# Attention with QK norm and a maxout FFN: two-part row loads, five turning products, regrouped values and an alternating spread in the first six head pairs, with the second pair's norms in the opening

## Chip, cores and metric

One Trainium2 chip, one core. The time is device microseconds of one execution; for each kernel the median of several executions is given. One further execution was profiled, and all rows below come from it. Engines: PE multiplies matrices (PEld loads its weights), DVE, ACT and POOL work on tiles in SBUF (DVE and ACT also in PSUM), SP only issues DMAs; ACT issues some too.

## The reference

```python
def _attn_ref(q, k, v, g_q, g_k):            # q, k, v: (8, 12, 448, 64) float32
    def rmsnorm(x, g):
        rms = np.sqrt(np.mean(x * x, axis=-1, keepdims=True) + 1e-06)
        return x / rms * g
    q_n, k_n = (rmsnorm(q, g_q), rmsnorm(k, g_k))
    scores = 1.0 / np.sqrt(q.shape[-1]) * np.matmul(q_n, k_n.transpose(0, 1, 3, 2))
    scores = scores - np.max(scores, axis=-1, keepdims=True)
    attn = np.exp(scores)
    attn = attn / (np.sum(attn, axis=-1, keepdims=True) + 1e-09)
    return np.matmul(attn, v).astype(np.float32)

def _moe_ref(x, w1, w2, w3, w_out):          # x: (3584, 768), all weights 768 x 768
    h = np.maximum(np.maximum(x @ w1, x @ w2), x @ w3)
    return (h @ w_out).astype(np.float32)
```

The attention's output, heads side by side, is the x of the second function, whose output is the result (3584 x 768, float32).

## The kernel before

The work goes by **pairs** of heads: 8 batches of 6 pairs, 48 pairs in all (index `g`), each with 2 x 448 = 896 rows of 64 numbers for q, k and v. The first six pairs (`PLAIN = 6`, batch 0) compute in float32; from the seventh on, operands are split into two float16 parts and turned by DMA. While the first ten pairs or so run, the weights are loaded (`raw`), decoded on DVE in three steps (L200, L204, L209), bounded by products on PE (`marks`, L265) and split (L293). From g = 6 on, the FFN's products (L841, L903) fill PE between the pairs' own work.

A pair is twelve `beat`s, and four chunks `c` of query rows: three of 128 rows for both heads (two banks of PSUM), and a last one with the 64 rows left of each head (`LEFT = 64`). The order of the instructions on every engine is the order in which the code is written (`manual_schedule`): `beat` calls the steps of the pairs g-1 to g+3, and `later(n, ...)` puts a step n beats on. Each engine takes its instructions strictly in that order and waits for the operands and buffers of the next one.

The path of one pair of the first six:

- `load_rows` (L350) brings the 896 rows as a tile of 128 partitions x 7 units. Units 0, 2, 4 are rows 0 to 383 (head 0), units 1, 3, 5 are rows 512 to 895 (head 1), and unit 6 is rows 384 to 511: the last 64 of head 0 on the lower half of the partitions, the first 64 of head 1 on the upper. Three DMAs do this. All are on SP's queue, but for k of the first pair, whose second and third are on ACT's. SP has eight semaphores for its DMAs in turn with those of ACT, so an issue waits for the landing of the eighth before it.
- `squares` (L404 ACT for the first two pairs, later POOL), `sum_squares` (L413, DVE), `inv_rms` (L423 and L427, POOL, a power of -0.5) give `ri`; `scale_rows` (L435, DVE for the first pair, later POOL) gives `kn` and `qn`.
- `turn_whole` (L490, L501) turns them on PE: three transposes of 128 x 128, head 0 on partitions 0 to 63 and head 1 on 64 to 127, then three products that put the rest beside them: head 1's first 64 columns stand ahead of the transposes' columns, head 0's last 64 behind them. `keep_whole` copies the result to `kt` (L513) and, times the gain, to `qt` (L517) on ACT.
- `scores` (L624) multiplies a chunk of qt by all of kt; `SHIFT` picks the 448 columns of each head. Two buffers `sc` exist, so the scores of chunk n+2 wait for the exponentials of chunk n.
- `row_max` (`nm`, L655, DVE), `softmax` (`e`, L671, ACT), `turn_plain` (L691, PE: e turned in four blocks of 112 keys), `keep_turned` (`pt`, L704, ACT), `add_values` (`av`, L801, PE: 4 blocks of 112 keys, the two heads alternating between the lower and the upper half of the output's partitions).
- `guard_sums`, `inverse_sums`, then `spread_sums` (L727, L733): eight products that spread each query row's 1/sum over the 64 partitions of its head; `keep_sums` copies that to `by` (L743, ACT), and `scale_plain` (L820, DVE) multiplies `av` by it.

`load_v` (L382) brings three pairs' values as one tile. In batch 0 partition p holds keys p, 112+p, 224+p, 336+p of each head, in pieces of 64 numbers, four DMAs a tile; `largest_v` (L543) sends the tile through PE once to bound it.

The code ahead of the first beat is the **opening**: it loads pairs 0 and 1 and the two gains, prepares pair 0 up to kt and qt, computes the gain's column (`column`, L1022; `gain_c`, L1025) and the constants of `prep_gain` (needed from the seventh pair on), and then pair 1's squares, sums, norms and scaling.

## Time and profile before

| | us |
|---|---|
| three timed executions | 1033.67, 1035.94, 1036.47 (median 1035.94) |
| profiled execution | 1033.57 |
| its span on the core | 1031.8 |
| PE busy | 988.9 (96%) |
| DVE busy | 697.5 (68%) |
| ACT busy | 622.8 (60%) |
| POOL busy | 598.5 (58%) |

In a row of a timeline stand the start, the duration, the engine, the line of the code, the operation, the tiles (written <- read), the shape, the number of instructions merged into the row, and in brackets how long the engine was idle before and who released it. PEclk is the share of PE's full clock that was granted. A float32 product is two passes, so `x6` of L727 are three products. A q behind an engine's name (SPq, ACTq) marks its DMA issues.

### The profile page before, as it was taken

What the parts mean: (1) busy time and instruction counts of PE and PEld (TensorE: products, weight loads), DVE (VectorE), ACT (ScalarE), POOL (GpSimd) and SP (SyncE); (2) the same over time, 40 slices, a digit from 0 to 9 for tenths busy, and PEclk for the clock granted to TensorE, in tenths of its full rate; (3) what the DMA queues carried; (4) which work ended last, traced back from release to release, by engine and by line L of the source; (5) the groups of instructions that cost most, each with busy time, mean ns of one, the idle gap of its engine ahead of it and who ended that gap; (6) DMA issues with size and microseconds to landing.
All of it is one profiled execution on the core that took longest, in us unless ns stands there. A gap on an engine that the chain in (4) does not pass through costs nothing.

```text
span 1031.8 us, 17413 instructions
## 1 busy us (share of the span) xinstructions
PE 988.9 (96%) x5988; PEld 530.6 (51%) x5988; DVE 697.5 (68%) x1343; ACT 622.8 (60%) x1419; POOL 598.5 (58%) x652
## 2 busy tenths in 40 slices
PE   5999789898899999999999999999999999999998
PEld 3655444444455555555555555555555555555555
DVE  4898989987676856776667767786777666760120
ACT  3787866667666676666665666666665766651111
POOL 5566676765766666756666576676675766410000
PEclk9999879999999999999999999999999999999999
DMA  8866698997999999999999899999999998861001
GB/s 200 202 178 172 165 204 164 177 166 134 209 173 171 167 182 210 168 172 151 221 171 188 152 216 181 177 169 180 193 168 169 179 201 145 135 104 59 1 1 62
DMA packets 524089, 165.99 MB, mean 161 GB/s; under 512 B 500321, under 2 KB 519777, under 8 KB 524001
## 3 DMA queue, kind: packets, MB, share of 16 engines
q1 hardware_dynamic: 460992, 148.89, 74.8%
q10 hardware_dynamic: 63008, 16.00, 8.7%
q8 instruction: 47, 0.77, 0.3%
q14 instruction: 42, 0.34, 0.1%
HBM read 53.35 MB, written 11.01 MB: 62 GB/s over the span
## 4 chain that ended last, share of the span: by engine, by line
PE 74%; DVE 2%; ACT 1%; DMA 1%; issue 1%; SPq 0%; ACTq 0%
PE acc L841 41%; PE acc L903 15%; PE av L812 8%; PE sc L633 8%; PE sc L640 1%; DVE pp L767 1%; DVE nm L655 1%; DMA pt<-pp 1%; ACT sc L671 0%; DVE w_sb L335 0%; DVE ss L413 0%; DMA out_dram<-osb 0%; SPq L786 0%; ACT w_sb L330 0%; ACT pp L757 0%
## 5 line engine op out<-in xcount | busy, mean ns | idle before, releaser
L841 PE MATMUL acc<-xt,w_sb 128*128 128x448 f16 x2592 | 516.8, 355 | 0.0
L841 PEld LDWEIGHTS <-w_sb 128*128 128x128 f16 x2592 | 252.5, 98 | 245.0 <-issue 16.8
L671 ACT ACTIVATE sc<-sc,nm 128x448 f32<-128x448 f32 x294 | 178.8, 608 | 197.0 <-DVE nm L655 192.5
L655 DVE TENSOR_REDUCE nm<-sc 128x2 f32<-128x896 f32 x192 | 186.3, 970 | 101.5 <-PE sc L640 51.4
L757 ACT ACTIVATE pp<-sc,rs 128x448 f16<-128x448 f32 x294 | 172.8, 633 | 77.9 <-issue 29.2
L767 DVE SCALAR_TENSOR_TENSOR pp<-sc,rs,pp 128x448 f16<-128x448 f32 x294 | 188.0, 675 | 3.3 <-ACT pp L757 3.2
L427 POOL TENSOR_TENSOR ri<-ri,half_neg 128x7 f32<-128x7 f32 x96 | 148.8, 1550 | 8.0
L903 PE MATMUL acc<-w_sb,ht 128*128 128x384 f16 x864 | 148.6, 327 | 0.0
L461 POOL TENSOR_TENSOR kp<-kn,kp 128x448 f16<-128x448 f32 x42 | 44.7, 1065 | 167.6 <-ACT kp L455 154.5
L633 PE MATMUL sc<-kt,qt 128*128 128x448 f16 x504 | 117.6, 356 | 10.4 <-DVE pp L767 7.7
L903 PEld LDWEIGHTS <-ht 128*128 128x128 f16 x864 | 83.8, 99 | 60.2 <-issue 5.8
L633 PEld LDWEIGHTS <-qt 128*128 128x128 f16 x504 | 48.8, 98 | 56.0 <-issue 6.9
L812 PE MATMUL av<-pt,vp 128*64 128x448 f16 x672 | 72.2, 355 | 0.7 <-DMA pt<-pp 0.6
L870 POOL COPY hx<-ht 128x128 f16<-128x128 f16 x48 | 15.3, 318 | 94.3 <-DVE ht L865 94.3
L413 DVE TENSOR_REDUCE ss<-sq 128x7 f32<-128x448 f32 x96 | 57.6, 601 | 11.4 <-ACT sq L404 8.3
L595 POOL TENSOR_TENSOR vp<-vr,vp 128x512 f16<-128x512 f32 x42 | 50.0, 1189 | 22.6 <-ACT vp L589 22.6
L750 DVE TENSOR_SCALAR rs<-sc 128x2 f32<-128x2 f32 (+1 forms) x168 | 26.2, 156 | 50.4 <-ACT sc L671 50.3
L827 DVE SCALAR_TENSOR_TENSOR xt<-av,xt 128x448 f16<-128x448 f32 x42 | 26.2, 623 | 49.0 <-ACT xt L826 49.0
L461 POOL TENSOR_TENSOR qp<-qn,qp 128x448 f16<-128x448 f32 x42 | 46.2, 1100 | 19.2 <-ACT qp L455 16.9
L855 DVE TENSOR_TENSOR m<-acc,m 128x448 f32<-128x448 f32 x48 | 29.6, 617 | 37.7 <-PE acc L841 37.5
L812 PEld LDWEIGHTS <-vp 128*64 128x64 f16 x672 | 35.0, 109 | 35.0 <-issue 15.5
L861 ACT ACTIVATE ht<-acc 128x448 f16<-128x448 f32 x48 | 26.2, 546 | 41.8 <-DVE acc L855 41.8
(130 smaller groups left out, 1181.4 us busy)
## 6 DMA issues: line engine op xcount, KB each, us to landing
raw<-in_moe_w_dram SPq DMA_DIRECT2D x18, 768.0 KB, 4.5
kt<-kt SPq DMA_DIRECT2D x84, 112.0 KB, 2.5
out_dram<-osb SPq DMA_DIRECT2D x24, 384.0 KB, 3.7
vr<-in_v_dram SPq DMA_DIRECT2D x42, 192.0 KB, 4.1
kr<-in_k_dram ACTq DMA_DIRECT2D x34, 224.0 KB, 3.3
qr<-in_q_dram ACTq DMA_DIRECT2D x34, 224.0 KB, 4.6
raw<-in_moe_w_out_dram SPq DMA_DIRECT2D x6, 768.0 KB, 5.0
vs<-vp SPq DMA_DIRECT2D x84, 48.0 KB, 2.1
```

Source lines behind the costliest of these rows:

```text
L413: nc.vector.tensor_reduce(sums[g % 2][:, KQ[what]], sq, axis=AX, op=ALU.add)
L427: nc.gpsimd.tensor_tensor(out=ri, in0=ri, in1=half_neg[:, at], op=ALU.pow)
L461: nc.gpsimd.tensor_tensor(out=parts[:, :, 1], in0=n, in1=parts[:, :, 0], op=ALU.subtract)
L595: nc.gpsimd.tensor_tensor(out=vp[:, 1], in0=values_of(g).rearrange("p h n d -> p (h n) d"), in1=vp[:, 0], op=ALU.subtract,)
L633: nc.tensor.matmul(sc[:, h, :S], qt[:, 4 * h + c], kt[:, n, keys[h]], start=n == 0, stop=n == 1,)
L655: nc.vector.tensor_reduce(nm[:, :n], sc[:, :n, :S], axis=AX, op=ALU.max, negate=True)
L671: nc.scalar.activation(to, sc[:, h, :S], AF.Exp, bias=nm[:, h:h + 1], accum_out=total,)
L757: nc.scalar.activation(pp[:, h, 0], sc[:, h, :S], AF.Copy, scale=rs[:, h:h + 1])
L767: nc.vector.scalar_tensor_tensor(out=pp[:, h, 1], in0=sc[:, h, :S], scalar=rs[:, h:h + 1], in1=pp[:, h, 0], op0=ALU.mult, op1=ALU.subtract,)
L812: nc.tensor.matmul(av[half, :S], values, pt[:, 7 * h + block, SHIFT[h]:SHIFT[h] + S], start=n == 0, stop=n == len(steps) - 1,)
L841: nc.tensor.matmul(acc[:, :S], wt[:, wp, c], xs[c][:, xp], start=(c == 0 and n == 0), stop=(c == NCT - 1 and n == 2),)
L903: nc.tensor.matmul(acc[:, :HW], lhs, wo_sb[:, f, wp, half * HW:(half + 1) * HW], start=(f == 0 and n == 0), stop=(f == NFT - 1 and n == 2),)
```

## The change

Six edits, all in the first six pairs or the opening. (1) `load_rows` uses two DMAs: units 0, 2, 4, 6 (rows 0 to 511) and units 1, 3, 5; the second part of the first pair's q goes to ACT's queue as that of k does. (2) `turn_whole` makes five products: three transposes to columns 0 to 383, and two products of 64 x 64 that turn unit 6 in its two halves to columns 384 to 447. Head 1's columns thus run 64 to 447, then 0 to 63; `qt` and `kt` are 448 wide and `scores` needs no shift. (3) `keep_whole` writes kt with its columns regrouped: column 4n+u goes to 112u+n. (4) `load_v` fits this for batch 0: partition p holds keys 4p to 4p+3 of a head, head 1's rotated by 64, in pieces of 256 numbers; three DMAs a tile. (5) `spread_sums` alternates between the two heads. (6) The opening: the second pair's squares and sums stand ahead of or between the first pair's scaling, its `inv_rms` behind the first pair's `keep_whole`, `prep_gain` behind that, and the column's products between the turning of k and of q.

```diff
@@ load_rows, load_q
         if g < PLAIN:
-            for h in range(2):
-                on[h].dma_start(out=t[:, h:6:2], in_=rows[:, 4 * h:4 * h + 3])
-            on[1].dma_start(out=t[:, 6], in_=rows[:, 3])
+            on[0].dma_start(out=t[:, 0:7:2], in_=rows[:, 0:4])
+            on[1].dma_start(out=t[:, 1:6:2], in_=rows[:, 4:7])
     def load_q(g):
-        load_rows(g, "qr", q, (nc.sync, nc.sync) if g < LOADS else (nc.scalar,))
+        first = (nc.sync, nc.sync if g else nc.scalar)
+        load_rows(g, "qr", q, first if g < LOADS else (nc.scalar,))
@@ load_v
         if b == 0:
-            for u in range(4):
+            wrap = KEYS - LEFT // 4
+            for h, to, of in (
+                (0, slice(0, KEYS), slice(0, S)),
+                (1, slice(0, wrap), slice(LEFT, S)),
+                (1, slice(wrap, KEYS), slice(0, LEFT)),
+            ):
                 nc.sync.dma_start(
-                    out=vr[:KEYS, :, u],
-                    in_=rows[:, u * KEYS:(u + 1) * KEYS].rearrange("h p d -> p h d"),
+                    out=vr[to, h::2].rearrange("p h u d -> p h (u d)"),
+                    in_=rows[h::2, of].rearrange("h (p u) d -> p h (u d)", u=4),
                 )
@@ turn_whole
-                turned[:, LEFT + c * P:LEFT + (c + 1) * P],
+                turned[:, c * P:(c + 1) * P],
                 n[:, 2 * c:2 * c + 2].rearrange("p h d -> p (h d)"), ident,
             )
-        last = n[:, 5:7].rearrange("p n d -> p (n d)")
-        lower, upper = HALVES
-        for to, of, rows in (
-            (slice(0, LEFT), last, upper),
-            (slice(LEFT + 3 * P, 512), last, lower),
-            (slice(LEFT + 3 * P, 512), n[:, 6], lower),
-        ):
+        for half in HALVES:
             nc.tensor.matmul(
-                turned[:of.shape[1], to], of, ident[:, rows],
-                start=True, stop=True,
+                turned[half, 3 * P:S], n[half, 6], ident[half, half], start=True, stop=True
             )
@@ keep_whole
-            t = t.rearrange("p a n -> p (a n)").bitcast(F32)[:, :512]
-            nc.scalar.copy(t, turned)
+            t = t.rearrange("p a n -> p (a n)").bitcast(F32)[:, :S]
+            nc.scalar.copy(
+                t.rearrange("p (u n) -> p n u", u=4),
+                turned[:, :S].rearrange("p (n u) -> p n u", u=4),
+            )
         else:
-            t = t.rearrange("p n r -> p (n r)").bitcast(F32)
-            nc.scalar.activation(t, turned, AF.Copy, scale=gain_c)
+            t = t.rearrange("p n r -> p (n r)").bitcast(F32)[:, :S]
+            nc.scalar.activation(t, turned[:, :S], AF.Copy, scale=gain_c)
@@ scores
-                if c < 3:
-                    to, cols = sc[:, h, :S], slice(LEFT + c * P, LEFT + (c + 1) * P)
-                else:
-                    to = sc[rows, 0, :S]
-                    cols = slice(0, LEFT) if h else slice(LEFT + 3 * P, 512)
+                to = sc[:, h, :S] if c < 3 else sc[rows, 0, :S]
                 nc.tensor.matmul(
-                    to, qt[rows, cols], kt[rows, SHIFT[h]:SHIFT[h] + S],
-                    start=True, stop=True,
+                    to, qt[rows, c * P:min((c + 1) * P, S)], kt[rows], start=True, stop=True
                 )
@@ spread_sums
-        for h, half in enumerate(HALVES):
-            for c in range(3):
+        for c in range(3):
+            for h, half in enumerate(HALVES):
                 first = LEFT * h + c * P
                 nc.tensor.matmul(
                     spread[half, first:first + P],
...
+        for h, half in enumerate(HALVES):
             first = 0 if h else 3 * P
@@ the opening
+    for g in range(2):
+        for what in "kq":
+            squares(g, what)
     for what in "kq":
-        squares(0, what)
-    sum_squares(0, "k")
-    inv_rms(0, "k")
-    sum_squares(0, "q")
-    inv_rms(0, "q")
+        sum_squares(0, what)
+        inv_rms(0, what)
     nc.vector.tensor_tensor(out=gain, in0=gains[:, 0], in1=gains[:, 1], op=ALU.mult)
+    sum_squares(1, "k")
     scale_rows(0, "k")
+    sum_squares(1, "q")
     scale_rows(0, "q")
+    turn_whole(0, "k")
     column = ps_m.tile([P, 512], F32, name="column", tag="m")
...
     nc.scalar.activation(gain_c, column[:, 0:1], AF.Copy, scale=1.0 / float(D) ** 0.5)
-    prep_gain()
-    for what in "kq":
-        turn_whole(0, what)
+    turn_whole(0, "q")
     for what in "kq":
         keep_whole(0, what)
-    for what in "kq":
-        squares(1, what)
-        sum_squares(1, what)
         inv_rms(1, what)
+    prep_gain()
     scale_rows(1, "k")
     scale_rows(1, "q")
```

Three places show how the instructions stand now. The first is DVE's opening, as a difference of the two programs; `ss_88` holds the sums of the even pairs, `ss_89` those of the odd ones, `kn` and `qn` are the scaled rows of the first pair (lines of the changed kernel are 8 higher there).

```order
 L144 MEMSET root 128x1
-L413 TENSOR_REDUCE ss_88<-sq 128x7 x2
+L421 TENSOR_REDUCE ss_88<-sq 128x7 x2
 L1016 TENSOR_TENSOR gain<-gains 128x64
-L435 TENSOR_TENSOR kn<-kr,ri 128x448
-L435 TENSOR_TENSOR qn<-qr,ri 128x448
+L421 TENSOR_REDUCE ss_89<-sq 128x7
+L443 TENSOR_TENSOR kn<-kr,ri 128x448
+L421 TENSOR_REDUCE ss_89<-sq 128x7
+L443 TENSOR_TENSOR qn<-qr,ri 128x448
 L172 TENSOR_REDUCE g_top<-gain 128x1
```

The two sums of the second pair, which stood behind all of `prep_gain`, stand ahead of kn and ahead of qn.

The second is POOL in the opening; `ri` are the norms' factors (from `ss_88` the first pair's, from `ss_89` the second's), and `even` belongs to `prep_gain`.

```order
-L427 TENSOR_TENSOR ri<-ri,half_neg 128x7
+L431 TENSOR_SCALAR ri<-ss_88 128x7
+L435 TENSOR_TENSOR ri<-ri,half_neg 128x7
+L431 TENSOR_SCALAR ri<-ss_88 128x7
+L435 TENSOR_TENSOR ri<-ri,half_neg 128x7
+L431 TENSOR_SCALAR ri<-ss_89 128x7
+L435 TENSOR_TENSOR ri<-ri,half_neg 128x7
+L431 TENSOR_SCALAR ri<-ss_89 128x7
+L435 TENSOR_TENSOR ri<-ri,half_neg 128x7
 L1005 TENSOR_TENSOR even<-even,root 128x1
-L423 TENSOR_SCALAR ri<-ss_89 128x7
-L427 TENSOR_TENSOR ri<-ri,half_neg 128x7
```

The second pair's four steps stand ahead of `even` now, and behind them follows the scaling of the second pair's rows, as before.

The third is PE at the spread of a pair's sums; the row behind it is the next pair's last chunk of scores.

```order
-L727 MATMUL spread<-ident,sum 64x128 x3
-L733 MATMUL spread<-ident,sum 64x64
-L727 MATMUL spread<-ident,sum 64x128 x3
-L733 MATMUL spread<-ident,sum 64x64
+L726 MATMUL spread<-ident,sum 64x128 x6
+L733 MATMUL spread<-ident,sum 64x64 x2
 L624 MATMUL sc<-kt,qt 64x448 x2
```

The six wide products stand together, lower and upper half of the output in turn, and the two small ones behind them.

## The prediction

> **What bounds the kernel now.** I read the page first, then busy time by stretch, then each engine's timeline over the first 130 us, where the change acts.
>
> ```profile
> 34.40:52.20 17.80, 17.41 (x130) 10.83 (x128) 13.94 (x25) 12.72 (x31) 9.47 (x10) 1.00 0.67 191
> 70.10:88.60 18.50, 16.68 (x116) 10.11 (x116) 17.43 (x28) 15.00 (x35) 11.12 (x10) 1.00 0.71 183
> 600.00:800.00 200.00, 200.00 (x1215) 105.08 (x1215) 142.02 (x281) 128.58 (x301) 130.70 (x148) 1.00 1.01 181
> ```
>
> After the length come busy times of PE, PEld, DVE, ACT, POOL, then PE's granted clock. Late in the program PE never rests and its order is fixed, so time saved early is kept to the end. The early pairs differ: the one at 34 us is PE's (17.41 of 17.8 busy); by 70 us DVE has 17.43 of 18.5, and a faster PE gains only what DVE still idles. Before both lies the opening, a chain of waits.
>
> **Opening: the first scores.** They start at 14.74, behind qt, which waits for the turning of qn:
>
> ```profile
> 2.51 0.45 ACTq L969 DMA_DIRECT2D gains<-in_g_k_dram  x1
> gains<-in_g_k_dram ACTq DMA_DIRECT2D x1, 32.0 KB, 5.4
> 3.03 0.90 SPq L358 DMA_DIRECT2D kr<-in_k_dram  x2
> kr<-in_k_dram SPq DMA_DIRECT2D x2, 96.0 KB, 5.2
> 7.60 0.58 ACT L404 ACTIVATE sq<-qr 128x448 f32<-128x448 f32 x1 [2.54 <-DMA kr<-in_k_dram]
> 8.20 0.62 DVE L413 TENSOR_REDUCE ss<-sq 128x7 f32<-128x448 f32 x1 [2.49 <-ACT sq L404]
> 8.74 0.22 DVE L1016 TENSOR_TENSOR gain<-gains 128x64 f32<-128x64 f32 x1
> 8.87 0.62 DVE L435 TENSOR_TENSOR kn<-kr,ri 128x448 f32<-128x448 f32 x1
> 11.17 0.62 DVE L435 TENSOR_TENSOR qn<-qr,ri 128x448 f32<-128x448 f32 x1 [1.68 <-POOL ri L427]
> 11.85 0.90 PE L490 MATMUL rows<-ident,qn 128*128 128x128 f32 x3 [0.25 <-DVE qn L435]
> 12.54 1.36 PE L501 MATMUL rows<-ident,qn 128*128 128x64 f32 x6
> 14.74 3.36 PE L624 MATMUL sc<-kt,qt 64*128 64x448 f32 x8 [0.84 <-ACT qt L517]
> ```
>
> Half of q(0) moves to ACT's queue and each load loses one DMA, so q(0) is squared before 7.60. That isn't the new limit, though: DVE now has two sums of the second pair between gain, kn and qn. The gain product waits for g_k, landed at 2.51+5.4 = 7.9; its issue stays, but 96 KB of rows rather than 32 KB stand ahead of it on that queue, so I put it at 8.2. Then DVE waits for k(1): landed from 3.03+5.2 = 8.2 on, its last part some 0.5 later. It is now issued over 1 us sooner but shares its time with the same gains; I take 8.4. ACT squares it (0.58) to 9.0, DVE sums (0.62) to 9.6, kn runs to 10.25, 0.75 **later** than its 9.49 before; the next sum ends at 10.85, qn at 11.45 against 11.79. POOL's ri for q, the old releaser, is done earlier, since its sum no longer waits for q.
>
> Then PE: 2.05 us of turning (11.85 to 13.90) becomes the three transposes (12.54-11.85 = 0.70) and, for L501's six passes in 1.36, four passes of half the width. At 1.36/6 each that is 0.9, if both halves of the array overlap and the narrower weights count 0.35; I take 0.45, which saves 0.9. Qt covers 64 columns fewer. The scores start at 13.4, **1.3 us earlier** (bounds -0.5, if k(1) lands at 10, to 2.2).
>
> **Opening: the second pair's norms.**
>
> ```profile
> 18.05 1.48 POOL L427 TENSOR_TENSOR ri<-ri,half_neg 128x7 f32<-128x7 f32 x1
> 20.49 0.90 PE L490 MATMUL rows<-ident,kn 128*128 128x128 f32 x3 [2.39 <-POOL kn L435]
> 22.48 1.86 PE L624 MATMUL sc<-kt,qt 64*128 64x448 f32 x4
> 18.92 0.20 ACT L671 ACTIVATION_READ_ACCUMULATOR e<-sc,nm 128x1 f32 x1
> 19.02 0.87 ACT L192 ACTIVATE raw<-raw 128x768 f32<-128x768 f32 x1
> 22.58 0.58 ACT L513 COPY kt<-rows 128x512 f32<-128x512 f32 x1 [2.69 <-PE rows L501]
> 24.27 1.09 PE L691 MATMUL turned<-ident,e 128*112 128x128 f32 x8
> 28.89 0.91 PE L543 MATMUL marks<-vr 112*128 112x128 bf16 x12
> ```
>
> PE idled 2.39 us for kn(1), which waited for ri of q(1), ready at 18.05+1.48 = 19.5. That ri now follows the second sum (10.85) by the two long POOL steps, so about 13.2; kn(1) then stands ready near 15, well before PE asks. What is late next? The third scores need the buffer that the first exponentials free (18.92+0.20 = 19.1, less 1.3 is 17.8); PE itself ends the scores at 18.1-1.3 = 16.8 and the rows at 17.95. So they start at 18.0 for 22.48, 4.5 earlier. ACT is next (raw 17.7 to 18.6, kt to 19.1, then the second exponentials); the turning starts at 18.0+1.8 = 19.8 for 24.27. DVE's decoding stands in the same stretch, so I take **4.0 us** for the whole opening. Bounds: 1.5 (k(1) late, POOL slow) to 5 (PE's clock is low here: four score passes take 1.86, later 1.02; it may rise sooner).
>
> Its DMAs: the weights' raw loads go out some 3 us sooner, ahead of k(2), and the values come in 1 KB pieces instead of 256 bytes. The second values' products stood at 28.89 and are now wanted at 24.9; if that tile lands late, PE waits there, at worst for all of the 4.0.
>
> **Spread and rows, per pair.**
>
> ```profile
> 36.39 3.23 PE L801 MATMUL av<-pt,vr 112*64 112x448 f32 x16
> 39.94 0.81 PE L501 MATMUL rows<-ident,qn 128*128 128x64 f32 x6
> 40.68 1.21 PE L265 MATMUL marks<-w_sb 128*128 128x128 bf16 x18
> 41.82 0.87 PE L727 MATMUL spread<-ident,sum 128*64 128x128 f32 x6
> 42.62 0.32 PE L733 MATMUL spread<-ident,sum 64*64 64x64 f32 x2
> 43.93 0.86 PE L543 MATMUL marks<-vr 128*128 128x128 bf16 x12
> ```
>
> Spread takes 41.82 to 43.93, 2.1 us; twelve passes of 128 columns are 1.6 of it, 0.80/6 = 0.13 each, all of one half of the output before the other. Does alternating help? L801 alternates halves: 3.23/16 = 0.20 us for a pass of 448 columns. At the spread's rate such a pass would take 0.13x448/128 = 0.46. So alternate halves overlap, about twofold. I take 0.7 for the twelve and 0.6 for the four small ones with one change of shape instead of three: 0.8 saved (bounds 0.2, where only the changes of shape go, and 1.1). L501 (39.94 to 40.68, 0.74) becomes two small products of 0.2 to 0.25 each by L733: 0.33 saved a tile (0.2 to 0.5).
>
> How much of it arrives is DVE's idle time in front of the step that PE releases:
>
> ```profile
> 41.93 0.29 DVE L172 TENSOR_REDUCE most<-marks 128x1 f32<-128x128 f32 x1 [0.82 <-PE marks L265]
> 44.83 0.29 DVE L172 TENSOR_REDUCE v_rows<-marks 128x1 f32<-128x128 f32 x1 [2.61 <-PE marks L543]
> 54.95 0.63 ACT L671 ACTIVATE e<-sc,nm 128x448 f32<-128x448 f32 x1 [0.81 <-DVE nm L655]
> 62.63 0.63 DVE L655 TENSOR_REDUCE nm<-sc 128x1 f32<-128x448 f32 x1 [1.67 <-PE sc L624]
> 70.16 1.02 PE L624 MATMUL sc<-kt,qt 64*128 64x448 f32 x4 [0.80 <-ACT e L671]
> 81.19 0.62 DVE L655 TENSOR_REDUCE nm<-sc 128x1 f32<-128x448 f32 x1 [0.77 <-PE sc L624]
> 88.69 1.55 PE L624 MATMUL sc<-kt,qt 64*128 64x448 f32 x4 [0.80 <-ACT e L671]
> 100.68 0.29 DVE L172 TENSOR_REDUCE v_rows<-marks 128x1 f32<-128x128 f32 x1 [2.14 <-PE marks L543]
> 120.40 0.62 DVE L655 TENSOR_REDUCE nm<-sc 128x1 f32<-128x448 f32 x1 [0.75 <-PE sc L624]
> ```
>
> Up to 45 us three tiles and a spread, 1.8 (DVE idles 3.4); q's tile and a spread, 1.13, at 62 and at 100; 0.8 at 81, capped by 0.77; 0.75 at 120, where no rows are left. K's tile of each pair ends before PE's own wait for ACT's e (0.80) and brings nothing; the sixth spread stands where DVE holds PE. Sum 1.8+1.13+0.8+1.13+0.75 = **5.6** (bounds 2 to 7).
>
> Costed at nothing: fewer row DMAs, since SP isn't what these steps wait for; the gain's preparation behind the norms, needed from the seventh pair only; and the kt copy. Its cover is ACT's idle time before e (0.81 at 54.95).
>
> One rule speaks against that copy. L192 works on every second word, 768 in 0.87 us against L513's 512 in 0.58: the same rate, so steps of 8 bytes cost nothing. The new copy writes at steps of 448 bytes. By the rows it takes 0.53 (448/512 of 0.58); I bound it at double, 1.1, mostly inside that idle time, so the sum falls by under 1.
> The Trainium skill, "SBUF — State Buffer", "Door 1: The DMA port swizzle", says that every access which crosses to a new 16-byte line pays a penalty, without its size. By that rule the copy is dearer than 0.53; no run here shows it yet.
>
> **Sum.** 4.0+5.6 = 9.6 off the profiled run's 1033.57 (span 1031.8 and 1.8 around it) is 1024.0; I take 1 back for a slower PE clock (rival A): 1025.0. The three timed runs have a median of 1035.94, 2.4 above the profiled one; I add about half of that: **1026**. This case alone: 1022 to 1029.
>
> **Rivals.**
> A. PE's clock. The scores at 88.69 took 1.55 where those at 70.16 took 1.02, and the window behind shows half the clock, after a stretch in which PE had work for 2.76 of 4 us:
>
> ```profile
> 85.00:89.00 4.00, 2.76 (x19) 1.70 (x17) 3.91 (x8) 4.00 (x10) 1.67 (x2) 1.00 0.90 206
> 89.00:92.40 3.40, 3.40 (x14) 1.84 (x12) 3.39 (x4) 1.54 (x4) 2.11 (x2) 0.51 1.01 238
> ```
>
> A PE that is done sooner waits longer for e, so the pairs at 52 and 70 may halve too. Price: 3.4 us at 0.51 lose up to 1.7 each. Two such pairs leave 9.6-3.4 = 6.2: 1028.6 with the added half. For: the waits grow. Against: the wait of 0.80 at 70.16 halved nothing. Chance 0.13.
> The Trainium skill, "TensorE: Matmul & The Clock Gate", "HAM oscillation — how this bites in real kernels", puts the limit at gaps of more than about 3.4 us; by that no pair would halve here and the sum would be 1 better. This trace disagrees: 85 to 89 holds only 1.24 us without work in all.
> B. The opening gives nothing: the gains stall k(1) beyond 10 us, or the values land late. 5.6-1 remain: 1030. For: k(1) took 5.2 us beside the gains. Against: it is issued sooner. Chance 0.1.
> C. Alternating doesn't overlap, so that the change doesn't do what it says: five spreads save 0.2 instead of 0.8, 3.0 less: 1029. Against it stands L801. Chance 0.06.
> D. **Slower**: the kt copy's scattered writes, on ACT ahead of e. Beyond 0.8 of cover each added microsecond counts in six pairs. To use up 8.6 and 3.1 more, a copy must take 0.58+0.8+11.7/6 = 3.3 us, 7 ns an element, where L192 shows about 1. At 4 us it would be 1040. Chance 0.04.
>
> **How the numbers follow.** Forecast 0.62, A 0.13, B 0.1, C 0.06, D 0.04, and 0.05 that more is gained, below 1021. The range, 1021 to 1031.5, holds the forecast, A, C and most of B. About 0.3%, 3.1 us, is what a measurement of this kernel can tell from no change, so below 1032.8 is faster: 0.85; within 0.1 (B's tail and losses that meet); slower 0.05.
>
> **What would show it.** First scores near 13.4 and third near 18; kn(0) on DVE behind gain and a sum, ending near 10.2; spread's eight products within 1.3 us; DVE's idle time at 81 gone; kt copies at 0.53. I am wrong if PE waits at the values' marks, if kn(0) ends after 11, or if half clock stands in every pair.

## The result, and the profile after

| | before | after |
|---|---|---|
| median of the runs, us | 1035.94 (1033.67 to 1036.47) | 1028.19 (1026.83 to 1031.45) |
| profiled execution, us | 1033.57 | 1028.1 |
| its span, us | 1031.8 | 1026.3 |

After over before is 0.9934, with a 95% interval of 0.9918 to 0.9951: 7.7 us between the medians, 5.5 between the two profiled spans. The forecast was 1026 in a range of 1021 to 1031.5.

First the busy times by stretch after the change, for the stretches that answer to 34.40, 70.10 and 600 before (length; PE, PEld, DVE, ACT, POOL busy; PE's granted clock; share of DMA; GB/s):

```profile
31.50:48.10 16.60, 15.54 (x126) 9.02 (x124) 14.39 (x25) 12.65 (x31) 9.51 (x10) 1.00 0.73 201
64.90:83.10 18.20, 14.86 (x112) 8.33 (x112) 18.06 (x28) 15.32 (x34) 11.84 (x10) 1.00 0.76 184
600.00:800.00 200.00, 200.00 (x1207) 104.81 (x1204) 142.53 (x280) 128.53 (x302) 132.33 (x150) 1.00 1.03 179
```

PE, busy in 17.41 of 17.8 us of the first stretch before, now rests for 1.1 of 16.6. In the second DVE is busy in 18.06 of 18.2, where it was 17.43 of 18.5. The late part is PE's without a gap, as it was: what is saved early is kept, and what is lost early too.

The opening in the timeline after the change (start, length, engine and line, what it does, and in brackets the idle time before it with what ended that):

```profile
9.30 0.22 DVE L1016 TENSOR_TENSOR gain<-gains 128x64 f32<-128x64 f32 x1 [2.86 <-DMA gains<-in_g_k_dram]
9.45 0.58 ACT L412 ACTIVATE sq<-kr 128x448 f32<-128x448 f32 x1 [3.65 <-DMA kr<-in_k_dram]
10.05 0.62 DVE L421 TENSOR_REDUCE ss<-sq 128x7 f32<-128x448 f32 x1 [0.53 <-ACT sq L412]
10.59 0.62 DVE L443 TENSOR_TENSOR kn<-kr,ri 128x448 f32<-128x448 f32 x1
11.65 0.61 DVE L443 TENSOR_TENSOR qn<-qr,ri 128x448 f32<-128x448 f32 x1
14.91 3.36 PE L624 MATMUL sc<-kt,qt 64*128 64x448 f32 x8 [0.79 <-ACT qt L521]
18.20 0.90 PE L498 MATMUL rows<-ident,kn 128*128 128x128 f32 x3
19.44 1.02 PE L624 MATMUL sc<-kt,qt 64*128 64x448 f32 x4
20.40 1.09 PE L690 MATMUL turned<-ident,e 128*112 128x128 f32 x8
22.58 0.85 PE L547 MATMUL marks<-vr 112*128 112x128 bf16 x12 [0.51 <-ACT pt L703]
26.54 0.73 PE L547 MATMUL marks<-vr 112*128 112x128 bf16 x10 [0.96 <-DMA vr<-in_v_dram]
```

Read it in three pieces. The **first scores** start at 14.91, 0.17 later than before: DVE stands 2.86 us for the gains and then for k(1)'s squares, so kn(0) ends at 11.2. PE then turns kn and multiplies for the column (12.50 to 12.87) before it turns qn, which is ready at 12.26 and is turned from 12.81 on. The **second pair's norms** are where the opening gains: PE no longer waits for kn(1) (18.20 has no bracket), and the turning of e starts at 20.40 for 24.27, 3.87 us earlier. Then **the values** take a part back: PE stands 0.96 us for the second values tile.

The first spread in the same timeline:

```profile
38.48 0.88 PE L726 MATMUL spread<-ident,sum 128*64 128x128 f32 x12
39.29 0.33 PE L733 MATMUL spread<-ident,sum 64*64 64x64 f32 x4
```

and all of DVE's waits over 0.2 us between 34 and 126 us after the change:

```profile
38.59 0.29 DVE L172 TENSOR_REDUCE most<-marks 128x1 f32<-128x128 f32 x1 [0.50 <-PE marks L265]
40.45 0.29 DVE L172 TENSOR_REDUCE v_rows<-marks 128x1 f32<-128x128 f32 x1 [1.57 <-PE marks L547]
57.08 0.62 DVE L654 TENSOR_REDUCE nm<-sc 128x1 f32<-128x448 f32 x1 [0.26 <-PE sc L624]
93.78 0.29 DVE L172 TENSOR_REDUCE v_rows<-marks 128x1 f32<-128x128 f32 x1 [0.66 <-PE marks L547]
```

Twelve passes take 0.88 where they took 1.7, and the whole spread runs from 38.48 to 39.55, 1.07 us for 2.11. DVE's waits of 1.67 at 62.63 and 0.77 at 81.19 are 0.26 and nothing.

So where did DVE's waits go? One row for the same 117 DVE instructions, before and after:

```profile
44.83:126.15 81.32, 73.32 (x492) 43.92 (x493) 74.52 (x117) 63.92 (x141) 50.55 (x40) 0.96 0.57 158
```

```profile
40.45:119.96 79.51, 68.32 (x482) 38.16 (x482) 77.28 (x117) 65.64 (x142) 53.89 (x42) 0.94 0.64 168
```

DVE was idle for 81.32-74.52 = 6.8 us and is now for 2.23: 4.6 us of waits went. But the same 117 instructions take 77.28 for 74.52, so that **2.8 us of the 4.6 came back as longer DVE work**, and the stretch is only 1.81 shorter. Set side by side, it is in five decoding steps of the weights, each longer by 0.6 to 0.9 (two others became shorter, by 0.46 and 0.28). The changed kernel's second profile (e12) has 2.4 for the 2.8. Two of the five with GpSimd's rows beside them, before:

```profile
62.50 0.93 POOL L435 TENSOR_TENSOR qn<-qr,ri 128x448 f32<-128x448 f32 x1
62.63 0.63 DVE L655 TENSOR_REDUCE nm<-sc 128x1 f32<-128x448 f32 x1 [1.67 <-PE sc L624]
64.17 0.94 DVE L204 SCALAR_TENSOR_TENSOR w_sb<-raw,w_sb 128x768 uint32<-128x768 uint32 x1
...
81.96 0.93 POOL L435 TENSOR_TENSOR qn<-qr,ri 128x448 f32<-128x448 f32 x1
83.71 1.02 DVE L293 SCALAR_TENSOR_TENSOR w_sb<-w_sb,w_up 128x768 f16<-128x768 f32 x1
```

and after:

```profile
58.36 0.94 POOL L443 TENSOR_TENSOR qn<-qr,ri 128x448 f32<-128x448 f32 x1
58.60 1.51 DVE L204 SCALAR_TENSOR_TENSOR w_sb<-raw,w_sb 128x768 uint32<-128x768 uint32 x1
...
76.83 1.65 POOL L443 TENSOR_TENSOR qn<-qr,ri 128x448 f32<-128x448 f32 x1
77.61 1.69 DVE L293 SCALAR_TENSOR_TENSOR w_sb<-w_sb,w_up 128x768 f16<-128x768 f32 x1
```

Before, the product for the queries had ended (63.43) when the decoding step began (64.17), because DVE had stood for PE. A faster PE lets DVE begin 58.60 beside the product of 58.36: 0.94 becomes 1.51. In the second place both stretch, 0.93 to 1.65 and 1.02 to 1.69. The maxima that read scores from PSUM (0.63 at 62.63, beside the same product) don't stretch. The Trainium skill, "SBUF — State Buffer", "Who interferes with whom", says that a DVE instruction with two SBUF inputs contends with a GpSimd instruction that reads SBUF, and that a reduce does not; these rows agree. It is the rule that spoke against this change and that the prediction left out. The two-input rule doesn't cover the decoding step at L200, which has one tensor input and stretches too (1.28 for 0.55 at 40.66, beside a product from 40.59 to 41.53).

The rows also show how. A decoding step that begins while a product runs ends a fixed time behind it, as if it waited for the product's end: 0.81 us behind 59.30 and 0.82 behind 78.48 in the rows after. In the 13 profiles up to 130 us that holds for 174 of 180 such steps with two inputs (0.81 to 0.82 us; in the other six the product is the longer one) and for all 32 of L200 (0.41 to 0.42). With no such product beside them the steps take 0.93 to 1.05 and 0.50 to 0.59. Which of the two becomes longer can hang on very little: in e4 the L200 step and the product both begin at 41.15, and the step takes its 0.55 and the product 1.34.

The last piece is **PE's clock**. The same wait of 2.50 us, for the same step, before and after:

```profile
203.60 0.93 PE L633 MATMUL sc<-kt,qt 128*128 128x448 f16 x4 [2.50 <-DVE pp L767]
```

```profile
195.99 0.93 PE L632 MATMUL sc<-kt,qt 128*128 128x448 f16 x4 [2.50 <-DVE pp L767]
```

and the busy times around it, cut at steps of 3.413 us, before:

```profile
198.29:201.70 3.41, 2.81 (x15) 1.27 (x13) 3.21 (x5) 1.63 (x4) 3.33 (x5) 1.00 0.84 148
201.70:205.12 3.42, 1.52 (x8) 0.80 (x9) 3.12 (x7) 2.21 (x6) 1.48 (x3) 1.00 0.78 147
```

and after:

```profile
193.46:196.87 3.41, 0.91 (x6) 0.50 (x6) 3.11 (x7) 1.58 (x5) 1.77 (x2) 1.00 0.66 135
196.87:200.29 3.42, 3.42 (x11) 1.37 (x9) 3.12 (x7) 3.06 (x7) 3.04 (x4) 0.50 0.72 134
```

In each of the 13 profiles of this study the half-clock stretches start whole multiples of 3.413 us apart. Cutting all 13 at that step from 27 to 400 us and counting PE's work (matmuls and weight loads together) in each window at full clock: with under 1.36 us of work the next window was at half clock in 56 of 56 cases, with over 2.2 in none of about 1180, and between them in 34 of 66. Before, a boundary cut the wait of 2.50; after, the whole of it fell into one window, which left 0.91 of work, and the next ran at 0.50. Where the boundaries fall moves the end by some 2 us: of the 12 profiles besides before, seven have a half-clock window near here (194.6 to 201.9) and lose 2.0 to 2.1 us between the rows 195.04 and 267.25 of the next table, and the other five change by under 0.1.

How much earlier than before each kernel stands, by the starts of the same maximum of scores on DVE (`nm`), in us (time of before, then time saved):

| before | after | same again | old opening | old spread | third raw later | no q product | sums later | values early | opening only |
|---|---|---|---|---|---|---|---|---|---|
| 24.44 | 2.84 | 2.56 | 0.30 | 2.87 | 1.87 | 1.99 | 2.18 | 3.59 | 2.01 |
| 31.86 | 3.02 | 2.64 | 0.29 | 2.27 | 2.94 | 3.07 | 2.50 | 4.65 | 1.12 |
| 49.70 | 4.13 | 3.62 | 1.42 | 2.66 | 4.37 | 4.08 | 3.21 | 6.08 | 0.42 |
| 67.55 | 5.13 | 4.60 | 2.40 | 3.06 | 5.35 | 5.29 | 4.36 | 7.07 | 0.42 |
| 86.11 | 5.43 | 4.90 | 2.54 | 3.06 | 4.95 | 6.28 | 2.30 | 7.36 | 0.43 |
| 106.50 | 6.12 | 5.61 | 3.56 | 3.42 | 5.07 | 7.02 | 1.26 | 8.13 | 0.79 |
| 126.15 | 6.19 | 5.55 | 3.60 | 3.38 | 4.98 | 7.20 | 1.45 | 8.31 | 0.82 |
| 195.04 | 7.61 | 6.96 | 4.54 | 6.29 | 5.95 | 8.74 | 2.86 | 9.78 | 2.37 |
| 267.25 | 5.47 | 4.83 | 4.54 | 4.27 | 5.95 | 6.63 | 0.76 | 7.66 | 0.25 |
| 923.25 | 5.52 | 5.60 | 4.85 | 4.20 | 6.28 | 6.80 | 0.90 | 7.70 | 0.65 |

Each column is one execution, and "same again" is the changed kernel in e12. With e3 and e4, which differ from it in one copy only and stand at 2.54 and 2.45 at 31.86 and at 5.07 and 6.11 at 126.15, it shows how far a column can be trusted: a difference of under 0.6 at 31.86, or 1.1 at 126.15, tells nothing. The gains land between 8.9 and 10.4 us in the profiles with the changed loads, and the half-clock windows, which begin at 65 us in e4 and at 84 in the first profile after, stand at other places each time. From 126 to 267 a column shows mostly in which windows its waits fell: from 6.19 the changed kernel gains 1.4 (before has two half-clock windows more there, at 143.7 and 160.7) and loses 2.1 (its own at 196.9).

### The profile page after: what moved, and what is told of

Its sections match the earlier page's. It is cut to its first block, busy times and chain, and to the rows that moved or that the text cites. A ratio compares the mean times of both kernels' runs of the same rounds, so it can differ in the third digit from the quotient of the medians.

```text
span 1026.3 us, 17342 instructions
## 1 busy us (share of the span) xinstructions
PE 977.5 (95%) x5964; PEld 519.3 (51%) x5964; DVE 700.7 (68%) x1343; ACT 624.6 (61%) x1419; POOL 600.8 (59%) x652
## 4 chain that ended last, share of the span: by engine, by line
PE 50%; DMA 1%; ACT 0%; DVE 0%; SPq 0%; issue 0%
PE acc L841 29%; PE acc L903 10%; PE av L812 5%; PE sc L632 5%; PE sc L639 1%; DMA pt<-pp 0%; DMA out_dram<-osb 0%; ACT osb L912 0%; DVE ss L421 0%; PE most L558 0%; SPq L786 0%; DVE rs L750 0%; DVE rs L754 0%
```

## Experiments

All times beside the kernel before, five rounds each; the ratio is to before. Two sets of the changed kernel itself (1028.19 and 1027.65, below) show what a median can tell: about 1 us.

| kernel | median, us | ratio, 95% interval |
|---|---|---|
| changed kernel | 1028.19 | 0.9934, 0.9918 to 0.9951 |
| e1 old opening | 1029.19 | 0.9948, 0.9934 to 0.9961 |
| e2 spread in halves | 1030.38 | 0.9958, 0.9945 to 0.9971 |
| e3 strided read | 1028.73 | 0.9945, 0.9931 to 0.9960 |
| e4 plain copy | 1028.47 | 0.9943, 0.9931 to 0.9955 |
| e6 third raw later | 1026.87 | 0.9924, 0.9909 to 0.9939 |
| e7 both | 1027.77 | 0.9931, 0.9915 to 0.9947 |
| e8 opening only | 1034.29 | 0.9991, 0.9981 to 1.0001 |
| e9 no q product | 1026.72 | 0.9923, 0.9907 to 0.9940 |
| e10 sums later | 1032.45 | 0.9975, 0.9962 to 0.9988 |
| e11 values early | 1025.99 | 0.9908, 0.9893 to 0.9922 |
| e12 same again | 1027.65 | 0.9923, 0.9909 to 0.9936 |

**e1, the old opening in the changed kernel.**

```diff
-    for g in range(2):
-        for what in "kq":
-            squares(g, what)
     for what in "kq":
-        sum_squares(0, what)
-        inv_rms(0, what)
+        squares(0, what)
+    sum_squares(0, "k")
+    inv_rms(0, "k")
...
+    for what in "kq":
+        squares(1, what)
+        sum_squares(1, what)
         inv_rms(1, what)
```

> The changed kernel with the old order of the opening alone; loads, turning, spread and values stay as changed. My account: the new order brings the third scores from about 21 us to 18.6 and the turning of e from about 23 to 20.4, but the second values tile lands at 26.4 and PE waits for it, so 1 to 1.5 us of this is lost again; with the old order PE comes to the values late enough and that wait is gone. So e1 should end 1 to 1.5 us after the changed kernel, near 1029.5. Rival 1, the opening's whole 3.9 us are kept to the end: near 1032. Rival 2, what the opening gains is all lost at the values: within 0.5 us of the changed kernel. First scores in e1: 13.5 to 14, ahead of the changed kernel's 14.9, since DVE has no sums of the second pair between the first pair's norms.

Its timeline:

```profile
14.44 3.36 PE L624 MATMUL sc<-kt,qt 64*128 64x448 f32 x8 [0.79 <-ACT qt L521]
21.43 1.86 PE L624 MATMUL sc<-kt,qt 64*128 64x448 f32 x4
23.23 1.95 PE L690 MATMUL turned<-ident,e 128*112 128x128 f32 x8
```

The median is 1.0 us above the changed kernel's (1.5 above its second set), as my account had it. First scores come 0.47 earlier than with the new order (expected 0.9 to 1.4; the gains, which DVE waits for, landed at 10.2 in this execution and at 9.2 in the changed kernel's), the turning 2.8 later. The new order is worth 2.7 us at 31.86 in the table and 2.6 at 126, and 2.2 and 1.5 beside the lowest of the kernels that should stand level with the changed one. At the end of this one profile 0.7 is left: the changed kernel's window at 196.9 took the rest, and e1 has none there. So the opening is worth between 1.0, by the medians, and 2.7. Rival 1 (3.9) falls; rival 2 (nothing) falls by the table, since the medians alone tell no more than 1 us.

**e2, the spread's products in the old order.**

```diff
-        for c in range(3):
-            for h, half in enumerate(HALVES):
+        for h, half in enumerate(HALVES):
+            for c in range(3):
                 first = LEFT * h + c * P
...
-        for h, half in enumerate(HALVES):
```

> The changed kernel with the spread's products in the old order, all of one half of the output and then the other. My account: twelve passes go from 0.81 back to about 1.6 us, the spread from 1.0 to 1.9 to 2.1; DVE idles again in front of the maxima of the values (about 0.8 in pairs 1, 2 and 3, less at 81 and 120), and the end comes 3 to 4 us later than in the changed kernel, near 1031.5. Rival 1, the order of the halves is nothing and the smaller number of changes of shape saved the time: spread near 1.0 as well, end within 0.5 us. Rival 2, DVE is the bound so closely that it hides most of it: spread 1.9, end only 1 us later.

```profile
39.16 0.87 PE L726 MATMUL spread<-ident,sum 128*64 128x128 f32 x6
39.96 0.32 PE L732 MATMUL spread<-ident,sum 64*64 64x64 f32 x2
```

These two rows come twice, so the spread is back at 2.1 us (39.16 to 41.27). Six wide passes in a row, with no change of shape between them, take 0.80 (39.16 to 39.96), as long as twelve in turns: order alone makes the difference, and rival 1 falls. The end is 2.2 us later by the medians (2.7 by the second set). In the table 2.8 us are missing at 126 (1.7 beside e3) of 5 x 1.04 that PE gained: my 3 to 4 was too much, rival 2's 1 too little.

**e3 and e4, the keys' copy.** e3 exchanges the loops, so that the writes are contiguous and the reads from PSUM are not; e4 copies without grouping.

```diff
-                t.rearrange("p (u n) -> p n u", u=4),
-                turned[:, :S].rearrange("p (n u) -> p n u", u=4),
+                t.rearrange("p (u n) -> p u n", u=4),
+                turned[:, :S].rearrange("p (n u) -> p u n", u=4),
```

> The changed kernel with the key copy's loops exchanged: contiguous writes, reads from PSUM at steps of four words. Theory W, the scattered writes (steps of 448 bytes) are what makes the copy 0.94 us: it falls to 0.53 to 0.6 here. Theory R, any access that isn't contiguous on either side costs as much: it stays at 0.85 to 1.0. Either way the copy lies mostly beside ACT's wait for DVE's nm, and I expect the end within 1 us of the changed kernel; if the copy is on the path in all six pairs, W would give 6 x 0.4 = 2.4 us less, near 1025.8.

> The changed kernel with the keys of the first six pairs copied as they stand, not grouped by four (so keys and values no longer belong together: that part of the computation is changed). This is the price of the grouping by itself. The copy should take 448/512 of the old 0.61, 0.53 us. Account: hidden, end within 1 us of the changed kernel. Rival: on the path in all six pairs, 2.4 us less, near 1025.8. If e3 stays at 0.9 and e4 ends earlier, the grouping costs what e4 shows.

The group of the copy in the changed kernel, in e3 and in e4 (busy us, mean ns of one):

```profile
L514 ACT COPY kt<-rows 128x448 f32<-128x448 f32 x6 | 5.6, 941 | 0.0
```

```profile
L514 ACT COPY kt<-rows 128x448 f32<-128x448 f32 x6 | 3.2, 533 | 0.0
```

```profile
L514 ACT COPY kt<-rows 128x448 f32<-128x448 f32 x6 | 3.2, 538 | 0.0
```

Theory W holds: it is the scattered writes that cost, 0.41 us a copy, and reads at steps of four words cost nothing. The medians (1028.73, 1028.47) are those of the changed kernel: six copies, 2.4 us of ACT's time, hidden as far as a median can tell (about 1 us).

**e6, the third raw load later.**

```diff
-    for _ in range(3):
+    for _ in range(2):
         load_raw()
...
             later(5, lambda: largest_v(i // 3))
+            if i == 3:
+                load_raw()
```

> The changed kernel with two of the three raw weight loads in the opening and the third issued behind the second values tile. Theory V (the second values tile lands late, at 26.4 us, because of what stands ahead of it on the transfers): it lands some 2 us earlier, the wait of 0.96 us in front of its marks goes, and the stages from 27 us on start about 1 us earlier than in the changed kernel (the maximum of the scores that starts at 28.84 there starts near 27.9). Rival: the tile's own transfer sets its landing; the wait stays at 0.8 to 1.0. At the end I expect 0 to 1.5 us less than in the changed kernel, 1027 to 1028.5, since PE's half-clock windows shift by as much.

```profile
26.21 0.86 PE L547 MATMUL marks<-vr 112*128 112x128 bf16 x12
```

No wait stands in front of the second values tile any more: by the records of its transfers it landed at 25.1 instead of 26.4. In this execution the gains landed 0.9 us later than in the first profile (10.1 for 9.2), so that the kernel is 1.0 behind at 24.44 and level at 31.86: 0.9 came back where the wait was. Theory V holds, with 0.9 for the 0.96; in the profiles with three raw loads in the opening and the changed order the tile landed between 26.4 and 27.3. The maximum itself stands at 28.91, since the gains were late (expected 27.9). What it is worth later isn't shown: at 126 this execution is 1.2 behind, as low as e3, and the median is 0.8 to 1.3 below the changed kernel, about what a median can tell.

**e7, the first pair scaled first, and the third raw load later.**

```diff
     for what in "kq":
         sum_squares(0, what)
         inv_rms(0, what)
+    scale_rows(0, "k")
+    scale_rows(0, "q")
     nc.vector.tensor_tensor(out=gain, in0=gains[:, 0], in1=gains[:, 1], op=ALU.mult)
     sum_squares(1, "k")
-    scale_rows(0, "k")
     sum_squares(1, "q")
-    scale_rows(0, "q")
 
     turn_whole(0, "k")
+    turn_whole(0, "q")
...
-    turn_whole(0, "q")
...
```

> As the run before (third raw load later), and VectorE scales the first pair's keys and queries before it forms the gain and the second pair's sums; PE turns both ahead of the gain's column. Theory G (the first scores were late because kn and qn stood behind a product that waited for the gains at 9.2 us and a sum that waited for k(1)): first scores at 12.7 to 13.2 instead of 14.9, the maximum at 28.84 near 26.5 to 27, and the end 1.5 to 2.5 us ahead of the changed kernel, near 1026. Rival 1: the second pair's norms, now later by 1.2 us, take the place of the first scores, and the maximum stands at 27.5 or later. Rival 2: the values tile again.

```profile
13.05 3.36 PE L624 MATMUL sc<-kt,qt 64*128 64x448 f32 x8 [1.51 <-ACT qt L521]
25.30 0.73 PE L547 MATMUL marks<-vr 112*128 112x128 bf16 x10 [1.03 <-DMA vr<-in_v_dram]
```

Theory G is right for the first scores, 13.05 for 14.91: kn and qn had stood behind DMAs that they don't need, and the turning of q behind the gain's column. The edit frees them from both at once, so it doesn't show the share of each. Rival 2 is right for what follows: PE is at the values earlier and waits for them as long as before, 1.03. The maximum stands at 27.66 (expected 26.5 to 27) and the median is not to be told from the changed kernel's. The profiled execution, the shortest of the six (1026.02), stands 1.2 ahead of the first profile after at 31.86 and 2.1 at 923.25.

**e11, the second values tile issued right behind the first**, besides e7's edits.

```diff
-            load_v(i // 3)
+            if i == 0:
+                load_v(0)
+                load_v(1)
             later(5, lambda: largest_v(i // 3))
```

> The kernel with the third raw load later and the first pair scaled first, and in addition the second values tile issued right behind the first, ahead of the fourth pair's keys and queries. Theory V: the tile lands near 23.3 instead of 25.2 us, the wait of 1.03 in front of its marks goes, and the maximum of scores that starts at 28.84 in the changed kernel and 27.66 with the two other edits starts near 26.6. Rival: the fourth pair's rows, now later, are waited for in its place (by GpSimd's squares near 28), and the maxima behind 40 us are no earlier. End near 1025.5 by V, near 1027 by the rival, each up to 2 us off with the half-clock windows.

```profile
12.88 3.36 PE L624 MATMUL sc<-kt,qt 64*128 64x448 f32 x8 [1.51 <-ACT qt L521]
18.61 1.02 PE L624 MATMUL sc<-kt,qt 64*128 64x448 f32 x4 [1.26 <-ACT e L670]
```

The tile landed at 22.5, no wait stands at either values tile, and the maximum starts at 27.21 (expected 26.6; the third scores now wait 1.26 for the first exponentials). The fourth pair's rows are not waited for: the saving grows from 4.65 at 31.86 to 6.08 at 49.70. The median is 9.4 us under that of before in its set and 1.7 under the changed kernel's; the table has it 2.1 to 2.2 ahead at 126 and at the end (2.8 and 2.1 beside "same again"). It is the fastest of all kernels here.

**e8, the new opening alone, in the kernel before.** Its edit is e1's, the other way.

> The kernel before with the new order of the opening alone; loads, turning, spread and values as before. If the parts add up, it gains what the changed kernel lost when it was given the old order, some 1 us at the end (near 1034), and 2.5 to 3.5 us at 27 us. Rival, the parts do not add up: before the change the second values tile landed at 28.9 us, later than in the changed kernel, so the opening alone is stopped there at once: turning of e near 21 to 22, but the maximum of scores that starts at 31.86 before starts no earlier than 31, and the end is within 0.5 us of before.

```profile
28.62 0.79 PE L543 MATMUL marks<-vr 112*128 112x128 bf16 x11 [1.39 <-DMA vr<-in_v_dram]
```

The turning starts at 21.97, 2.3 us earlier than before, but PE then waits 0.27 and 1.39 for a values tile that lands at 28.5 here, and 0.4 is left at 49.70. At the end 0.65 by the profile and 1.1 by the medians, an interval that reaches 1.0001. With the changed loads the tile lands at 26.4 to 27.3, and there the same opening is worth 2.2 to 2.7 at 49.70. So at 49.70 the parts don't add up, as the rival had it, though the maximum came at 30.74 (it had 31) and its end (0.5) was too little. At the end this can't be told: the opening alone and all the rest (e1) gain 1.1 and 5.8 by the medians, both together 7.7. Which of the loads' two edits brings the tile earlier was not tried.

**e9, without GpSimd's product for the queries of pairs 2 to 5.**

```diff
         rows, ri = s.pop(what + "r"), s["ri"][:, KQ[what]]
+        if what == "q" and 2 <= g < PLAIN:
+            s["qn"] = rows
+            s.pop("ri")
+            return
```

> The changed kernel without GpSimd's product that normalizes the queries of pairs 2 to 5 (counted from 0; left out of the computation: these queries go on as they were loaded). Theory P: VectorE's decoding steps at 40.66, 58.60 and 77.61 are longer than before the change (1.28, 1.51, 1.69 us for 0.55, 0.94, 1.02) because the faster PE lets them start beside this product, which fell into VectorE's waits before. Without it they take 0.55, 0.95 and 1.0, and the stages behind 81 us start 1.5 to 2 us earlier than in the changed kernel. Rival: they are longer for ScalarE's or PE's sake, and stay so; stages within 0.5 us. End: 1 to 2 us less, if the half-clock windows don't move.

```profile
40.95 0.55 DVE L200 TENSOR_SCALAR w_sb<-raw 128x768 uint32<-128x768 uint32 x1
58.20 0.94 POOL L447 TENSOR_TENSOR kn<-kr,ri 128x448 f32<-128x448 f32 x1
58.65 1.29 DVE L204 SCALAR_TENSOR_TENSOR w_sb<-raw,w_sb 128x768 uint32<-128x768 uint32 x1
77.44 1.00 DVE L293 SCALAR_TENSOR_TENSOR w_sb<-w_sb,w_up 128x768 f16<-128x768 f32 x1
```

1.28 falls to 0.55 and 1.69 to 1.00. The one that stays long, 1.29, now runs beside the product for the keys, which came 0.7 later here. So the length follows GpSimd's product wherever it falls: theory P for the cause, and the rival falls. The size came out at or below the lower end of the 1.5 to 2 that I expected: from level at 31.86 the kernel is 0.85 ahead of the changed one at 86.11 and 1.0 at 126 (1.4 and 1.65 beside "same again"). Part of it is lost at once, since behind the step at 40.95 DVE waits for PE twice, 0.15 us each, which it didn't in the changed kernel. Of the 2.8 us of longer DVE work 1.4 are gone: 75.90 us for the same 117 instructions.

**e10, the same work, later.**

```diff
+            sums_at, inv_at, scale_at = ((5, 8), (7, 9), (8, 10)) if n < PLAIN else ((2, 5), (5, 7), (8, 9))
-            if i in (2, 5):
-                sum_squares(n, "kq"[i // 3])
+            if i in sums_at:
+                sum_squares(n, "kq"[sums_at.index(i)])
...
```

> The changed kernel, all of it computed, with both sums of squares of pairs 2 to 5 three steps later on VectorE, so that GpSimd's product for the keys stands where the one for the queries follows now and the one for the queries runs some 3 us later, beside VectorE's long maximum of scores in PSUM (1.08 us), which shows no stretch beside GpSimd. Theory P: the three decoding steps fall back to 0.55 to 1.0 us, the stages behind 81 us start 1 to 2 us earlier. Rival: the products meet other decoding steps there and stretch them as much; stages within 0.5 us of the changed kernel.

```profile
66.55 0.55 POOL L278 TENSOR_TENSOR w_up<-most,root 128x1 f32<-128x1 f32 x1
67.13 0.15 DVE L283 COPY w_most<-w_up 128x1 f32<-128x1 f32 x1 [1.35 <-POOL w_up L278]
```

A miss, and neither theory's: the steps that it meant did fall back (0.93 to 1.00 from 59.93 to 61.73 and at 80.55; one beside the moved product, at 47.56, takes 1.20), but behind the product on GpSimd's queue stands `w_up`, and DVE waits 1.35 us for it, in two pairs. GpSimd is late there too: its `ri` step, 0.21 us in the opening, begins at 59.91 beside three decoding steps, takes 2.83 and ends with the last of them. The kernel is 4.7 us behind the changed one at 126 (3.6 beside e3) and 4.3 by the medians. I had not asked what stands behind the moved instruction on its queue.

**e12, the changed kernel again.**

> The changed kernel itself once more, unaltered. Theory W: PE's clock is decided in windows of 3.413 us whose start has no fixed place in the program; a wait of 2.5 us halves the clock of the next window if it lies in one window and not if a boundary cuts it. Then this profile shows its half-clock windows at other times than 84.2, 101.3, 121.8, 135.4, 196.9, 241.3 and 268.6, but all of them again whole multiples of 3.413 apart, and the span differs from 1026.3 by up to 2 us for that reason alone. Rival: the windows stand where the program waits most, the same in each execution: the same seven times to 0.3 us, the span within 0.5.

Half-clock stretches start at 85.0, 102.1, 122.6, 136.2, 197.7 and 242.0, again whole multiples of 3.413 apart. They stand 0.7 to 0.8 later than the first time while the program stood only 0.3 to 0.7 later, and the one at 268.6 is missing; 0.55 us are won back there. The span is 1026.3 both times, as the rival had it. So theory W is right on the grid, but the places are steadier than it had it. That long waits decide which windows are hit, and the grid only those near the limit, fits both runs; two executions don't show it. At 126.15 this run of the same kernel stands 0.64 behind the first.

## Why the prediction was right, and which steps were not

The time fell into the range and into the forecast's own 1022 to 1029, 2.2 us above the point, although two of the three signs that were named for being wrong came true: what they cost, and the longer DVE work below, was less than the terms that held, and the range was 10 us wide. On the profiled spans the sum was 9.6 less 1 for the clock, 8.6, and 5.5 was measured: 3.0 (opening) + 3.2 (pairs) - 0.7 (windows). The last hangs on the clock's grid: e12 reaches the same span by 2.6 + 2.9 + 0.0. Step by step:

- **First scores**, 13.4 and 1.3 earlier: wrong. They start at 14.91. The mis-sized terms are the landings: gains 8.2, measured 9.2, and k(1) 8.4, measured 9.4, by the records of the transfers. With them kn(0) ends at 11.2 and not 10.25, which is the first of the two signs, and qn at 12.26 and not 11.45: 0.8 of the 1.5. Another 0.55 is a wait that the sum left out: it let PE turn qn at once, but PE is still at kn and the column then, and starts at 12.81. e7, freed from both transfers and with the column behind, starts the scores at 13.05.
- **Second pair's norms**: right. Turning was put at 19.8 and came at 20.40, although the first scores were 1.5 late, since PE's clock rose sooner (four score passes at 19.44 take 1.02, not 1.86); that was the reason given for the upper bound.
- **Values late**, kept as a mishap (rival B) and as a bound: it happened, in part. PE waits 0.96 us for the second tile, the second sign, and the opening's 3.87 end as 3.02 at 31.86. e6 and e11 show it from the other side.
- **Opening, 4.0**: 3.0 in the trace, 2.6 in e12's.
- **Spread, 0.8 saved, and rows, 0.33**: right in mechanism and too small: 1.04 a spread, and the turning of a tile's last columns 0.33 where it was 0.81. Rival C falls with e2.
- **What arrives of it, 5.6**: the step that failed. The rule (DVE's idle time ahead of the step that PE releases) gave the waits nearly: from 44.83 on 4.6 us of them went, where its terms for that stretch are 3.8. What the prediction left out is that GpSimd used these waits. Its products now run beside DVE's decoding, which takes 2.8 us more; 3.2 us arrive (3.02 at 31.86 to 6.19 at 126.15; 2.9 in e12). e9 shows the cause, and with four of these products left out half of the size.
- **The keys' copy, 0.53**: measured 0.94, inside the bound of 1.1. The Trainium skill, "SBUF — State Buffer", "Door 1: The DMA port swizzle", with its penalty for every new 16-byte line, pointed the right way, and e3 shows that the writes are the cause. Rated at nothing on the path: right, as far as the medians of e3 and e4 can tell. Rival D falls.
- **Clock** (rival A): no more windows than before: counted in units of 3.413 us, nine before 280 us in both profiles. They are not tied to a gap of some length either: 2.05 us without work (3.41 less 1.36) were always enough if they lay in one window. The Trainium skill, "TensorE: Matmul & The Clock Gate", "What's actually happening", gives a free-running window of 3413 ns, and these traces agree with it; the limit of 3.4 us for a gap, weighed in the prediction, does not hold here: the wait of 2.50 was enough. The third sign, half clock in every pair, did not come.
- **The added microsecond** for the median: the profiled run after (1028.1) lies at its median, so that nothing was to be added there; the sum was 3.1 too low on the profiled run and is 2.2 too low on the median.

Two errors of size on one side, the late landings of the opening and DVE's longer work, took 3.4 us of 9.6. The sign was safe because the two large mechanisms, the norms and the spread, held.

## What to carry to other kernels

Before counting an engine's idle time as gain, look at who works in it: GpSimd's products ran at 0.93 us there, and in five places beside DVE's decoding steps they cost DVE 0.6 to 0.9 each. A chain that is shortened hands its gain to the next transfer in the same queue; move that transfer with it (e11), and before moving an instruction look at what stands behind it on its own queue (e10). Compare two kernels of this kind by where they stand before the clock windows begin to differ, not by their ends alone.

## What had not been expected of the hardware

- PE's clock is set for whole windows of 3.413 us that keep their grid through the program. Under 1.36 us of PE work in one halved the next in 56 of 56 cases, over 2.2 in none of about 1180.
- A DVE decoding step (128 x 768, 32 bits) that begins while a GpSimd product (128 x 448, f32) runs ends 0.81 to 0.82 us behind it with two tensor inputs (174 of 180 cases) and 0.41 to 0.42 with one (32 of 32). Alone such steps take 0.93 to 1.05 and 0.50 to 0.59.
- Six f32 passes of 128 columns into one half of the output and then six into the other take 2 x 0.80 us from start to next start; taken in turns, 0.81 for all twelve.
- An ACT copy of 448 words from PSUM takes 0.94 us with writes at steps of 448 bytes and 0.53 with reads at steps of 16 bytes or none.
